# Routing gates of the next expert, split over the first and second layer of a mixture-of-experts kernel

## The chip, the cores and the metric

One core of one Trainium2 chip. The core has a matrix engine (TensorE, with its weight loads shown apart as PEld), VectorE (DVE), ScalarE (ACT), GpSimd (POOL) and SyncE (SP), which each work through their own queue in order and wait for each other through semaphores. The metric is the device time of one execution in microseconds; the median over the runs is compared.

## The reference

Two blocks follow each other. The first is a gated linear recurrence over 768 steps for 4 x 8 heads of width 48; its result, 3072 tokens of 384 numbers, is the input of the second, a router over 8 experts with one expert for each token:

```
xn = x / (np.linalg.norm(x, axis=-1, keepdims=True) + 1e-06)
logits = xn @ en.T / tau
expert_idx = np.argmax(logits, axis=1)
probs = np.exp(logits - logits.max(-1, keepdims=True))
probs /= probs.sum(-1, keepdims=True) + 1e-09
gate_w = probs[np.arange(N), expert_idx]
for e in range(E):
    mask = expert_idx == e
    h = np.maximum(x[mask] @ w1[e], 0.0)
    out[mask] = gate_w[mask, None] * (h @ w2[e])
```

w1 is 384 x 1024 and w2 is 1024 x 384 for each expert. The gate of a token is the softmax value of its largest logit. Since the largest shifted logit is 0, the gate is 1 over the sum of the exponentials. All is float32.

## The kernel before

The first part (up to some 165 us) runs the recurrence in 24 chunks of 128 tokens, computes each token's unnormalised logits, and writes each token's row (384 numbers, 8 logits, its index) to a table in DRAM that is sorted by expert. The part that matters here is the second: the loop over the 8 experts (`run(i)`, then `run_extra(i)`), each with up to three blocks of 128 rows, and a half block of 64 where an expert has more rows than that.

**Rows and weights.** Ahead of `run(i)`, SP fetches the weights of expert i+2 and the rows of expert i+2 into one of three row buffers (`xg_s`). So the rows that `run(i)` prepares, those of expert i+1, were fetched one expert earlier.

**First layer of experts 1 to 7** (`first_layer_blocks`, L995). Three blocks of rows are multiplied by fifteen products of pre-mixed weights and rows in place of eighteen (a Strassen-like scheme). TensorE runs a product into one of four PSUM banks; VectorE adds the bank to a hidden block (`add`, L1019), or ScalarE copies it (L1025, L1027, L1029, L1044, L1046) and applies the relu (L1022). Several products accumulate on a bank that a copy has read in between. Four times (`between`), TensorE transposes a block of the next expert's rows and ScalarE copies it to `xT` (L842, L846). Meanwhile GpSimd mixes the next expert's first weights (`mix_first_weights`, L965), ten operations of 128 x 512.

**Second layer.** The third block is multiplied plainly (`second_layer`, L904, sixteen instructions) and scaled by its gate on ScalarE (L907). The first two blocks are done together in seven products (`second_layer_pair`, L1065), each eight instructions at L1081, on mixed hidden blocks s1 to s4 (`mix_hidden`, L940) and mixed weights t1 to t4 (`mix_weights`, L929). ScalarE reads the first product out of its bank with the gate as a scale (L1093); the third product accumulates on the same bank, so TensorE waits for that reading. Further outputs are read by ScalarE at L1097, L1099 and L1106 and by VectorE in `gated` (L1088). GpSimd scatters the results to the output (L817).

**Rows of the next first layer** (`mix_first_rows`, L967): thirteen VectorE operations that mix the transposed rows of expert i+1.

**Gates of the next expert** (`gates`, L848, through `prepare_gates`, L881). ScalarE squares each block of rows with a running sum (L855, four times) and takes the root (L856). VectorE takes the largest logit (L858), masks the token index (L862, L863), forms the row to scatter to (L864), shifts the logits (L868), adds 1e-6 to the root and inverts it (L869, L870), and multiplies (L871). ScalarE takes Exp (L872). VectorE sums, adds 1e-9 and inverts (L873 to L875). The root and Exp each need a load of ScalarE's function table (L856 and L872, ACT_TABLE_LOAD). The whole is issued behind the last relu of the first layer and the last transposed copy; where it then comes on each engine is left to the scheduler of the language.

**The order of the work.** The program is given to a scheduler that places the instructions of each engine by priority and readiness. Where an order matters, the kernel writes it out: `turn_of(calls)` makes what follows issue behind the calls, `by_dve` chains a call on VectorE to the one before, and `pe_turn` does so on TensorE. ScalarE has no such chain. What the scheduler made of it, on ScalarE in `run(i)` for experts 1 to 6: copies and relus with the four transposed copies between, c21's relu behind the fourth of them, c22's relu, four squares, table load, root, L907, table load, Exp, L1093, L1097, L1099, L1106. On VectorE: the adds, s3, the five operations on the logits, s1, s2, s4, the thirteen row mixes, L869, L870, L871, the sum and what follows it, with `gated` and the next expert's weight mixes t1 to t4 between.

Expert 0 takes another path (its first 256 rows are done early, and a single block is left), and expert 7 prepares no gates.

Of the kernel before, what the change touches and what calls it, by code (L numbers as in the profile page):

```python
# [22 lines left out]
def bc(ap, shape, axis):  # L23
    return ap.unsqueeze(axis).to_broadcast(shape)
# [3 lines left out]
def kernel(  # L28
# [12 lines left out]
    nc = tc.nc  # L41
    B, H, S, D = q.shape
# [115 lines left out]
    def slots(i):  # L158
        return [(t, P) for t in range(blocks_run(i))] + [(blocks_run(i), HALF)]
# [625 lines left out]
    with ExitStack() as c3:  # L785
# [51 lines left out]
        def turn(xg, xT, n, by=None):  # L837
# [7 lines left out]
            pe[:] = [done]  # L845
            return by(xT, px[:, :, 0:n])  # L846

        def gates(xg, gate, col, n, has=None):  # L848

            shp = [P, n, E]  # L850
            l = xg[:, :, LG : LG + E]
            sq = yp.tile([P, NC + 1, 1], FP32, name="gsq")[:, 0:n]
            for t in range(n):
                x2 = yp.tile([P, DM], FP32, name="gx2", bufs=1)
                nc.scalar.activation(x2, xg[:, t, 0:DM], AF.Square, accum_out=sq[:, t])  # L855
            nc.scalar.activation(sq, sq, AF.Sqrt)  # L856
            top = yp.tile([P, NC + 1], FP32, name="gtop")[:, 0:n]
            nc.vector.tensor_reduce(top.unsqueeze(2), l, axis=AX.X, op=ALU.max)  # L858
            none = yp.tile([P, NC + 1, 1], FP32, name="none")[:, 0:n]
            token = xg[:, :, TK : TK + 1]  # L860
            if has is not None:
                nc.vector.tensor_tensor(token, token, has.unsqueeze(2), ALU.mult)  # L862
            nc.vector.tensor_scalar(none, token, 1.0, float(FAR), ALU.is_lt, ALU.mult)  # L863
            nc.vector.scalar_tensor_tensor(  # L864
                out=col.unsqueeze(2), in0=token, scalar=-1.0, in1=none, op0=ALU.add, op1=ALU.add
            )
            sh = yp.tile([P, NC + 1, E], FP32, name="gsh")[:, 0:n]
            nc.vector.tensor_tensor(sh, l, bc(top, shp, 2), ALU.subtract)  # L868
            nc.vector.tensor_scalar(sq, sq, 1e-6, None, ALU.add)  # L869
            nc.vector.reciprocal(sq, sq)  # L870
            nc.vector.tensor_tensor(sh, sh, sq.to_broadcast(shp), ALU.mult)  # L871
            nc.scalar.activation(sh, sh, AF.Exp)  # L872
            nc.vector.tensor_reduce(gate.unsqueeze(2), sh, axis=AX.X, op=ALU.add)  # L873
            nc.vector.tensor_scalar(gate, gate, 1e-9, None, ALU.add)
            return nc.vector.reciprocal(gate, gate)  # L875

        def prepare(i, t, by=None):
            _, n = slots(i)[t]
            return turn(xg_s[i % NXG][:, t], xT_s[i % 2][:, :, t * P : t * P + n], n, by)

        def prepare_gates(i):  # L881
            n = len(slots(i))
# [31 lines left out]

        dve = []

        def by_dve(call, *args):
            with turn_of(dve):
                dve[:] = [call(*args)]  # L919
            return dve[0]  # L920

        def pe_turn():
            return turn_of(pe)
# [13 lines left out]

            return [hT[:, j * FT // 2 : (j + 1) * FT // 2, t * P : (t + 1) * P] for j in range(2)]

        def mix_hidden(hT):  # L940

            (a11, a12), (a21, a22) = (hidden(hT, t) for t in range(2))
            s1, s2, s3, s4 = (hT_m[:, k] for k in range(4))
            for to, x, y, op in (
                (s3, a11, a21, ALU.subtract), (s1, a21, a22, ALU.add),
                (s2, s1, a11, ALU.subtract), (s4, a12, s2, ALU.subtract),
            ):
                by_dve(nc.vector.tensor_tensor, to, x, y, op)

        def halves_w1(w1_t):  # L950

# [40 lines left out]
            v.tensor_tensor(x14, one(b3, 0), x7, ALU.subtract)  # L992
            v.tensor_tensor(x15, one(b1, 1), x6, ALU.add)

        def first_layer_blocks(w1_t, hT, between):  # L995
# [12 lines left out]
            A, B, C, D = (grid(j) for j in (2, 1, 3, 0))  # L1008

            def product(to, left, right, start, stop):  # L1010
                with pe_turn():
                    for f in range(n):
                        pe[:] = [nc.tensor.matmul(  # L1013
                            to[:, f], lhsT=left[:, f * P : (f + 1) * P], rhs=right,
                            start=start and f == 0, stop=stop, skip_group_check=True,
                        )]

            def add(c, p):
                by_dve(nc.vector.tensor_tensor, c, p, c, ALU.add)  # L1019

            def relu(c, p):
                return nc.scalar.activation(c, p, AF.Relu)  # L1022

            product(A, a22, x1, True, False)
            nc.scalar.copy(c21, A)  # L1025
            product(B, g2, y1, True, False)
            nc.scalar.copy(c12, B)  # L1027
# [36 lines left out]

        def second_layer_pair(w2_t, hT, gate, col):  # L1065
# [24 lines left out]
                )  # L1090

            product(a, a11, b11, True, False)
            nc.scalar.mul(u[:, 0], a, g0)  # L1093
# [3 lines left out]
            nc.scalar.mul(u[:, 1], a, g0)  # L1097
            product(d, s1, t1, True, False)
            nc.scalar.mul(u[:, 2], d, g1)  # L1099
# [6 lines left out]
            done_pair[:] = pe[0], nc.scalar.mul(y1[:, 0:m], a, g1)  # L1106
            done_pair.append(scatter(y1, col[:, 1:2]))

        def half_block(w1_t, w2_t, xT, gate, col):
# [31 lines left out]
        def run(i):  # L1141
# [7 lines left out]
            dve[:] = [] if pair else ready  # L1149
            if pair:  # L1150
                mix_weights(w2_t)
                left = list(range(len(nxt)))
                rest = []

                def between():
                    if left:
                        rest[:] = [prepare(i + 1, left.pop(0), nc.scalar.copy)]

                done = first_layer_blocks(w1_t, hT, between)
                if nxt:  # L1160
                    turned = rest[0]
                mix_hidden(hT)
            else:
                for f in range(FT):
                    done = first_layer(w1_t, hT, xT[:, :, 0:n], f, n)
                    if f % 2 == 1 and f // 2 < len(nxt):
                        turned = prepare(i + 1, f // 2)
            if nxt:
                if pair:
                    mix_first_weights(i + 1, nc.gpsimd.tensor_tensor)  # L1170
                with turn_of(dve):
                    mix_first_rows(i + 1)
            if nxt:
                with tc.issue_after(done.ins), tc.issue_after(turned.ins):
                    prepare_gates(i + 1)
            else:

                with turn_of(done_pair):
                    drained.append(nc.gpsimd.drain())
            gate, col = gt_s[i % NG], sx_s[i % NG]  # L1180
            for t in range(2 if pair else 0, blocks_run(i)):
                sent = second_layer(
                    w2_t, hT[:, :, t * P : (t + 1) * P], gate[:, t : t + 1], col[:, t : t + 1],
                    nc.scalar.mul if pair else nc.vector.tensor_scalar_mul,
                )
            if not pair:

# [114 lines left out]
```

## Time and profile before

| | |
|---|---|
| median of 14 runs | 443.21 us (441.22 to 444.58) |
| the profiled execution | 443.46 us |
| its span on the core | 441.6 us |
| granted TensorE clock, mean | 0.979 |
| TensorE matmul busy | 409.6 us, 93% |
| VectorE busy | 285.1 us, 65% |
| ScalarE busy | 196.6 us, 45% |
| GpSimd busy | 222.0 us, 50% |
| expert loop | from about 165 us on |

All times are microseconds from the start of the span unless marked ns. A line of a group reads: line, engine, operation, output and inputs with shapes, how often, then busy time and mean ns of one, then the idle time of that engine just ahead and what ended it. A line of the timeline reads: start, duration, engine, line, operation, and in brackets the idle time ahead and its releaser. The granted clock is the share of full speed that the throttle left TensorE.

### The profile page before, as it was taken

To read this page: it belongs to the slowest core of one execution; us is meant where nothing else is said; L and a number is where in the kernel's file an instruction comes from. 1 tells how busy PE (TensorE), PEld (TensorE's weight loads), DVE (VectorE), ACT (ScalarE), POOL (GpSimd) and SP (SyncE) were. 2 spreads that over 40 slices of the span, in tenths; PEclk is the share of its full clock that TensorE was granted. 3 is DMA by queue.
4 is the path that set the end of the run, shared out by engine and by line. 5 is a ranking of instruction groups with operands and counts; after the bars stand their busy time and mean duration, and the time that the engine had idled before them with its cause. 6 is when DMAs were issued, how large, how long until landed. Compare 5 with 4: busy or idle time off the path is not lost. (4 is left out here: it accounts for less than half of the span.)

```text
span 441.6 us, 11748 instructions
## 1 busy us (share of the span) xinstructions
PE 409.6 (93%) x4570; PEld 363.2 (82%) x4570; DVE 285.1 (65%) x634; ACT 196.6 (45%) x433; POOL 222.0 (50%) x287
## 2 busy tenths in 40 slices
PE   7999999999999999999789889989979997998995
PEld 6798898889889776798689689789959987987984
DVE  7898687797897158636634944951683396397440
ACT  4455454545455344536314614712551471562331
POOL 7546767676655468139216615702831580681101
PEclk9999999999999999999989989989999998999999
DMA  9999999999989326873028009106401900100101
GB/s 140 152 166 150 191 190 189 193 173 205 213 251 387 121 86 185 316 252 124 15 94 296 17 17 340 41 0 242 143 18 50 331 2 16 39 1 16 38 15 40
DMA packets 119375, 60.22 MB, mean 136 GB/s; under 512 B 102287, under 2 KB 113816, under 8 KB 119312
## 3 DMA queue, kind: packets, MB, share of 16 engines
q1 hardware_dynamic: 115208, 49.14, 47.1%
q0 software_dynamic: 3728, 10.16, 6.5%
q8 instruction: 43, 0.70, 0.7%
q14 instruction: 20, 0.16, 0.1%
q10 hardware_dynamic: 376, 0.05, 0.1%
HBM read 49.69 MB, written 11.45 MB: 138 GB/s over the span
## 5 line engine op out<-in xcount | busy, mean ns | idle before, releaser
L817 POOL DMA_INDIRECT out_dram<-y,sx x25 | 26.0, 1040 | 127.2 <-DVE y L1088 64.9
L919 DVE TENSOR_TENSOR hT<-pq,hT 128x512 f32<-128x512 f32 x63 | 43.5, 692 | 52.8 <-PE pq L1013 51.0
L1013 PE MATMUL pq<-xT_m,w_m 128*128 128x128 f32 x560 | 67.8, 277 | 0.0
L1013 PEld LDWEIGHTS pq<-xT_m,w_m 128*128 128x128 f32 x560 | 65.3, 193 | 0.3 <-issue 0.3
L1081 PE MATMUL pq<-w_m,hT_m 128*128 128x192 f32 x168 | 35.8, 381 | 16.5 <-ACT u L1093 16.5
L1081 PEld LDWEIGHTS pq<-w_m,hT_m 128*128 128x128 f32 x168 | 33.9, 227 | 18.3 <-ACT u L1093 18.3
L507 POOL TENSOR_TENSOR qs<-qc,a 128x512 f32<-128x512 f32 x24 | 30.7, 1278 | 35.8 <-DVE a L503 24.2
L904 PE MATMUL pyo<-w,hT 128*128 128x384 f32 x128 | 42.6, 486 | 0.0
L965 POOL TENSOR_TENSOR w_m<-w_m,w 128x512 f32<-128x512 f32 x30 | 41.6, 1393 | 1.4
L1013 PE MATMUL pq<-xT_m,w 128*128 128x128 f32 x280 | 39.3, 281 | 2.4 <-PEq L1199 1.9
L1022 ACT ACTIVATE hT<-hT 128x512 f32<-128x512 f32 x35 | 22.1, 631 | 42.9 <-DVE hT L919 42.5
L1013 PEld LDWEIGHTS pq<-xT_m,w 128*128 128x128 f32 x280 | 35.7, 196 | 3.9 <-issue 3.6
L904 PEld LDWEIGHTS pyo<-w,hT 128*128 128x128 f32 x128 | 23.7, 190 | 14.8
L479 DVE TENSOR_TENSOR_SCAN r<-pa,inr 128x511 f32<-128x511 f32 x24 | 29.2, 1215 | 6.0 <-PE pa L194 5.1
L503 DVE TENSOR_TENSOR_SCAN a<-pa,ini 128x512 f32<-128x512 f32 x24 | 29.4, 1223 | 1.1
L313 POOL DMA_INDIRECT xs<-x,dest x24 | 24.3, 1013 | 8.2 <-issue 4.2
L191 PE MATMUL pyx<-sm,vt 128*64 128x128 f32 x384 | 26.5, 279 | 0.5 <-issue 0.5
L191 PE MATMUL sc<-qs,kr 64*64 64x128 f32 x768 | 26.5, 275 | 0.0
L919 DVE TENSOR_TENSOR w_m<-w 128x768 f32<-128x768 f32 x14 | 13.3, 952 | 20.2 <-PE pq L1081 20.2
L965 POOL TENSOR_TENSOR w_m<-w 128x512 f32<-128x512 f32 x12 | 15.3, 1275 | 19.6 <-PE pq L1013 19.6
L191 PEld LDWEIGHTS pyx<-sm,vt 128*64 128x64 f32 x384 | 20.6, 136 | 5.5 <-issue 5.5
L191 PEld LDWEIGHTS sc<-qs,kr 64*64 64x64 f32 x768 | 20.7, 132 | 4.0 <-issue 3.0
(215 smaller groups left out, 872.1 us busy)
## 6 DMA issues: line engine op xcount, KB each, us to landing
w<-in_moe_w_dram SPq DMA_DIRECT2D x16, 1536.0 KB
kt<-in_k_dram SPq DMA_DIRECT2D x24, 192.0 KB
qt<-in_q_dram SPq DMA_DIRECT2D x24, 192.0 KB
vt<-in_v_dram SPq DMA_DIRECT2D x24, 192.0 KB
xg<-xs SPq DMA_DIRECT2D x22, 196.5 KB
at<-in_alpha_dram SPq DMA_DIRECT2D x24, 168.0 KB
xg<-xs SPq DMA_DIRECT2D x8, 98.2 KB
at<-in_alpha_dram SPq DMA_DIRECT2D x24, 22.5 KB
```

Source lines behind the costliest of these rows:

```text
L191: last["pe"] = nc.tensor.matmul(*args, **kwargs)
L313: ins = nc.gpsimd.indirect_dma_start(out=xs, out_offset=bass.IndirectOffsetOnAxis(ap=rows, axis=0), in_=x, in_offset=None, bounds_check=E ...
L479: nc.vector.tensor_tensor_scan(r[:, L - 2 :: -1], pa[:, L - 1 : 0 : -1], inr[:, L - 2 :: -1], 1.0, ALU.mult, ALU.add,)
L503: d["a_scan"] = by_dve = nc.vector.tensor_tensor_scan(a, pa, ini, 0.0, ALU.mult, ALU.add)
L507: by_pool = nc.gpsimd.tensor_tensor(qs.rearrange("p n t -> p (n t)"), d["qc"], a, ALU.mult)
L817: ins = nc.gpsimd.indirect_dma_start(out=out, out_offset=bass.IndirectOffsetOnAxis(ap=col, axis=0), in_=y, in_offset=None, bounds_check=N - 1,
L904: pe[:] = [nc.tensor.matmul(py, lhsT=hT[:, f], rhs=w2_t[:, f], start=(f == 0), stop=(f == FT - 1),)]
L919: dve[:] = [call(*args)]
L965: by(to, x, y, op)
L1013: pe[:] = [nc.tensor.matmul(to[:, f], lhsT=left[:, f * P : (f + 1) * P], rhs=right, start=start and f == 0, stop=stop, skip_group_check=Tr ...
L1022: return nc.scalar.activation(c, p, AF.Relu)
L1081: pe[:] = [nc.tensor.matmul(to, lhsT=left[:, f], rhs=right[:, f], start=start and f == 0, stop=stop and f == n - 1, skip_group_check=True,)]
```

## The change

`gates` is taken apart into four functions, and in experts 1 to 6 they are called at four places:

- `gates_logits`: the five operations on the logits (largest, mask, index, shift). They are issued on VectorE ahead of the first layer's adds, behind the weight mixes t1 to t4.
- `gates_square`: one squared block. The four are issued on ScalarE within the first layer: behind the first transposed copy, behind c12's relu, and two behind the third transposed copy.
- `gates_norm`: root, addition, inverse, product, Exp. It is issued in `mix_hidden` between s1 and s2; on ScalarE that is behind c22's relu and ahead of L907.
- `gates_end`: sum, addition, inverse. It is issued behind s4 and ahead of the row mixes.

A chain `by_act` writes out ScalarE's order in `run(i)` for experts 1 to 7: the copies, relus, transposed copies, squares, root, Exp and the outputs of the second layer issue as the program lists them. With it the fourth transposed copy comes behind c21's relu. Expert 0 and the early rows keep the old sequence, through a `gates` that calls the four in turn.

```diff
+        def gates_logits(xg, col, n, has=None, by=freely):
...
+            by(v.tensor_reduce, top.unsqueeze(2), l, axis=AX.X, op=ALU.max)
...
+                by(v.tensor_tensor, token, token, has.unsqueeze(2), ALU.mult)
+            by(v.tensor_scalar, none, token, 1.0, float(FAR), ALU.is_lt, ALU.mult)
...
+            by(v.tensor_tensor, sh, l, bc(top, shp, 2), ALU.subtract)
+            return sh, yp.tile([P, NC + 1, 1], FP32, name="gsq")[:, 0:n]
+
+        def gates_square(xg, known, t, by=freely):
+            x2 = yp.tile([P, DM], FP32, name="gx2", bufs=1)
+            by(nc.scalar.activation, x2, xg[:, t, 0:DM], AF.Square, accum_out=known[1][:, t])
+
+        def gates_norm(known, n, by=freely, by_act=freely):
+            sh, sq = known
+            shp = [P, n, E]
+            by_act(nc.scalar.activation, sq, sq, AF.Sqrt)
+            by(nc.vector.tensor_scalar, sq, sq, 1e-6, None, ALU.add)
+            by(nc.vector.reciprocal, sq, sq)
+            by(nc.vector.tensor_tensor, sh, sh, sq.to_broadcast(shp), ALU.mult)
+            by_act(nc.scalar.activation, sh, sh, AF.Exp)
+
+        def gates_end(gate, known, n, by=freely):
+            sh, _ = known
+            by(nc.vector.tensor_reduce, gate.unsqueeze(2), sh, axis=AX.X, op=ALU.add)
+            by(nc.vector.tensor_scalar, gate, gate, 1e-9, None, ALU.add)
+            return by(nc.vector.reciprocal, gate, gate)
...
+        def by_act(call, *args, **kwargs):
+            with turn_of(act):
+                act[:] = [call(*args, **kwargs)]
+            return act[0]
...
-        def mix_hidden(hT):
+        def mix_hidden(hT, between):
...
+            by_dve(v.tensor_tensor, s3, a11, a21, ALU.subtract)
+            by_dve(v.tensor_tensor, s1, a21, a22, ALU.add)
+            between()
+            by_dve(v.tensor_tensor, s2, s1, a11, ALU.subtract)
+            by_dve(v.tensor_tensor, s4, a12, s2, ALU.subtract)
...
             product(D, a13, x11, True, True)
-            nc.scalar.copy(c11, D)
+            by_act(nc.scalar.copy, c11, D)
             between()
+            squares()
             product(A, f2, y2, False, False)
...
             relu(c12, c12)
+            squares()
             product(B, q7, x7, False, False)
-            nc.scalar.copy(c13, B)
+            by_act(nc.scalar.copy, c13, B)
             product(C, q10, x10, True, False)
-            nc.scalar.copy(c23, C)
+            by_act(nc.scalar.copy, c23, C)
             between()
+            squares()
+            squares()
...
             product(a, a11, b11, True, False)
-            nc.scalar.mul(u[:, 0], a, g0)
+            by_act(nc.scalar.mul, u[:, 0], a, g0)
...
                 mix_weights(w2_t)
...
+                if nxt:
+                    known = begin_gates(i + 1, by_dve)
...
+                def norm():
+                    if nxt:
+                        gates_norm(known, len(nxt), by_dve, by_act)
+
+                first_layer_blocks(w1_t, hT, between, squares)
+                mix_hidden(hT, norm)
                 if nxt:
-                    turned = rest[0]
-                mix_hidden(hT)
+                    gates_end(gt_s[(i + 1) % NG][:, 0 : len(nxt)], known, len(nxt), by_dve)
...
-            if nxt:
+            if nxt and not pair:
                 with tc.issue_after(done.ins), tc.issue_after(turned.ins):
                     prepare_gates(i + 1)
```

More of the change, by code (lines that the diff above doesn't have):

```diff
@@ L846, in turn, with freely @@
             return by(xT, px[:, :, 0:n])
+        def freely(call, *args, **kwargs):
+            return call(*args, **kwargs)
         def gates(xg, gate, col, n, has=None):
+            known = gates_logits(xg, col, n, has)
+            for t in range(n):
+                gates_square(xg, known, t)
+            gates_norm(known, n)
+            return gates_end(gate, known, n)
+        def gates_logits(xg, col, n, has=None, by=freely):
+            v = nc.vector
             shp = [P, n, E]
             l = xg[:, :, LG : LG + E]
[L852 to L856, printed above, removed]
             top = yp.tile([P, NC + 1], FP32, name="gtop")[:, 0:n]
-            nc.vector.tensor_reduce(top.unsqueeze(2), l, axis=AX.X, op=ALU.max)
+            by(v.tensor_reduce, top.unsqueeze(2), l, axis=AX.X, op=ALU.max)
             none = yp.tile([P, NC + 1, 1], FP32, name="none")[:, 0:n]
@@ L861, in gates @@
             if has is not None:
[L862 to L865, printed above, removed]
+                by(v.tensor_tensor, token, token, has.unsqueeze(2), ALU.mult)
+            by(v.tensor_scalar, none, token, 1.0, float(FAR), ALU.is_lt, ALU.mult)
+            by(
+                v.scalar_tensor_tensor,
+                out=col.unsqueeze(2), in0=token, scalar=-1.0, in1=none, op0=ALU.add, op1=ALU.add,
             )
             sh = yp.tile([P, NC + 1, E], FP32, name="gsh")[:, 0:n]
[L868 to L875, printed above, removed]
+            by(v.tensor_tensor, sh, l, bc(top, shp, 2), ALU.subtract)
[16 more added lines that the diff above has]
+            return by(nc.vector.reciprocal, gate, gate)
         def prepare(i, t, by=None):
@@ L879, in prepare, with begin_gates @@
             return turn(xg_s[i % NXG][:, t], xT_s[i % 2][:, :, t * P : t * P + n], n, by)
+        def begin_gates(i, by):
+            n = len(slots(i))
+            return gates_logits(
+                xg_s[i % NXG][:, 0:n], sx_s[i % NG][:, 0:n], n, used[:, i, 0:n], by
+            )
         def prepare_gates(i):
@@ L915, with by_dve @@
         dve = []
-        def by_dve(call, *args):
+        act = []
+        def by_dve(call, *args, **kwargs):
             with turn_of(dve):
-                dve[:] = [call(*args)]
+                dve[:] = [call(*args, **kwargs)]
             return dve[0]
+        def by_act(call, *args, **kwargs):
+            with turn_of(act):
+                act[:] = [call(*args, **kwargs)]
+            return act[0]
         def pe_turn():
@@ L938, in hidden @@
             return [hT[:, j * FT // 2 : (j + 1) * FT // 2, t * P : (t + 1) * P] for j in range(2)]
-        def mix_hidden(hT):
+        def mix_hidden(hT, between):
             (a11, a12), (a21, a22) = (hidden(hT, t) for t in range(2))
             s1, s2, s3, s4 = (hT_m[:, k] for k in range(4))
[L944 to L948, printed above, removed]
+            v = nc.vector
+            by_dve(v.tensor_tensor, s3, a11, a21, ALU.subtract)
[3 more added lines that the diff above has]
+            by_dve(v.tensor_tensor, s4, a12, s2, ALU.subtract)
         def halves_w1(w1_t):
@@ L993, in mix_first_rows, with first_layer_blocks @@
             v.tensor_tensor(x15, one(b1, 1), x6, ALU.add)
-        def first_layer_blocks(w1_t, hT, between):
+        def first_layer_blocks(w1_t, hT, between, squares):
             (a11, a12, a13), (a21, a22, a23) = halves_w1(w1_t)
@@ L1021, in relu @@
             def relu(c, p):
-                return nc.scalar.activation(c, p, AF.Relu)
+                return by_act(nc.scalar.activation, c, p, AF.Relu)
             product(A, a22, x1, True, False)
-            nc.scalar.copy(c21, A)
+            by_act(nc.scalar.copy, c21, A)
             product(B, g2, y1, True, False)
-            nc.scalar.copy(c12, B)
+            by_act(nc.scalar.copy, c12, B)
             product(D, a13, x11, True, True)
-            nc.scalar.copy(c11, D)
+            by_act(nc.scalar.copy, c11, D)
             between()
+            squares()
             product(A, f2, y2, False, False)
@@ L1096, in second_layer_pair @@
             product(a, s2, t2, False, False)
-            nc.scalar.mul(u[:, 1], a, g0)
+            by_act(nc.scalar.mul, u[:, 1], a, g0)
             product(d, s1, t1, True, False)
-            nc.scalar.mul(u[:, 2], d, g1)
+            by_act(nc.scalar.mul, u[:, 2], d, g1)
             product(a, s3, t3, False, False)
@@ L1105, in second_layer_pair @@
             product(a, a22, t4, False, True)
-            done_pair[:] = pe[0], nc.scalar.mul(y1[:, 0:m], a, g1)
+            done_pair[:] = pe[0], by_act(nc.scalar.mul, y1[:, 0:m], a, g1)
             done_pair.append(scatter(y1, col[:, 1:2]))
@@ L1151, in run, with squares @@
                 mix_weights(w2_t)
-                left = list(range(len(nxt)))
-                rest = []
+                left, late = list(range(len(nxt))), list(range(len(nxt)))
+                if nxt:
+                    known = begin_gates(i + 1, by_dve)
                 def between():
                     if left:
-                        rest[:] = [prepare(i + 1, left.pop(0), nc.scalar.copy)]
-                done = first_layer_blocks(w1_t, hT, between)
+                        prepare(i + 1, left.pop(0), lambda *args: by_act(nc.scalar.copy, *args))
+                def squares():
+                    if late:
+                        gates_square(xg_s[(i + 1) % NXG], known, late.pop(0), by_act)
+                def norm():
[3 more added lines that the diff above has]
+                mix_hidden(hT, norm)
                 if nxt:
-                    turned = rest[0]
-                mix_hidden(hT)
+                    gates_end(gt_s[(i + 1) % NG][:, 0 : len(nxt)], known, len(nxt), by_dve)
             else:
@@ L1172, in run @@
                     mix_first_rows(i + 1)
-            if nxt:
+            if nxt and not pair:
                 with tc.issue_after(done.ins), tc.issue_after(turned.ins):
                     prepare_gates(i + 1)
-            else:
+            if not nxt:
                 with turn_of(done_pair):
@@ L1183, in run @@
                     w2_t, hT[:, :, t * P : (t + 1) * P], gate[:, t : t + 1], col[:, t : t + 1],
-                    nc.scalar.mul if pair else nc.vector.tensor_scalar_mul,
+                    (lambda *args: by_act(nc.scalar.mul, *args)) if pair
+                    else nc.vector.tensor_scalar_mul,
                 )
```

## The prediction

> **What bounds the kernel now.** I read the page first. TensorE is busy for 409.6 of 441.6 us (93%), so what can be won is its idle time and its slow time. Next came the list of who waited for whom on TensorE, longest first:
>
> ```profile
> PE pq L1081 <- ACT u L1093: 16.5, 6, 2.9
> PE pq L1013 <- PEq L1199: 1.9, 1, 1.9
> ```
>
> One wait holds 16.5 us: six times, 2.9 us at most, at the second layer's products (L1081), until ScalarE has read the first product out of its bank (L1093). Third, the groups by shape on ScalarE tell why ScalarE is late there:
>
> ```profile
> L872 ACT ACTIVATE gsh<-gsh 128x32 f32<-128x32 f32 x7 | 1.6, 229 | 19.4 <-DVE gsh L871 19.4
> ```
>
> ScalarE sat idle for 19.4 us ahead of the gates' Exp, for VectorE's multiplication L871. Fourth, the timeline of one expert (its second-layer pair starts at 323.50 us) shows the chain; columns are start, duration, engine, line:
>
> ```profile
> 323.50 2.76 PE L1081 MATMUL pq<-w,hT 128*128 128x192 f32 x16
> 324.30 1.28 ACT L872 ACT_TABLE_LOAD   x1
> 324.88 0.42 DVE L979 TENSOR_TENSOR xT_m<-xT 128x256 f32<-128x256 f32 x1
> ...
> 327.71 0.28 DVE L993 TENSOR_TENSOR xT_m<-xT,xT_m 128x128 f32<-128x128 f32 x1
> ...
> 328.32 0.19 DVE L871 TENSOR_TENSOR gsh<-gsh,gsq 128x32 f32<-128x32 f32 x1
> 328.55 0.23 ACT L872 ACTIVATE gsh<-gsh 128x32 f32<-128x32 f32 x1 [2.96 <-DVE gsh L871]
> 328.68 0.40 ACT L1093 ACTIVATE u<-pq,gt 128x192 f32<-128x192 f32 x1
> 329.14 4.17 PE L1081 MATMUL pq<-w_m,hT_m 128*128 128x192 f32 x24 [2.87 <-ACT u L1093]
> ```
>
> ScalarE issues in order: Exp stands ahead of L1093 and waits for three small VectorE operations that stand behind thirteen row mixes (L979 to L993). Last, the windows of this stage, from the first product of the pair (L1081) to the start of the next first layer, for experts 1 to 7; columns are length, busy time and count of PE, PEld, DVE, ACT, POOL, granted clock, DMA:
>
> ```profile
> 211.71:225.63 13.92, 11.04 (x57) 10.75 (x56) 9.12 (x28) 3.25 (x6) 1.54 (x2) 0.88 0.03 12
> 249.28:263.19 13.91, 11.04 (x57) 10.75 (x56) 9.08 (x28) 3.25 (x6) 1.51 (x2) 0.88 0.04 15
> 283.45:297.37 13.92, 11.04 (x57) 10.75 (x56) 9.10 (x28) 3.25 (x6) 1.49 (x2) 0.88 0.04 15
> 323.50:335.78 12.28, 9.41 (x57) 9.04 (x56) 9.09 (x28) 3.25 (x6) 1.29 (x1) 1.00 0.04 16
> 362.07:375.98 13.91, 11.04 (x57) 10.75 (x56) 9.09 (x28) 3.25 (x6) 1.37 (x2) 0.88 0.03 13
> 396.24:407.80 11.56, 9.41 (x58) 9.05 (x56) 8.46 (x26) 3.25 (x6) 1.29 (x2) 1.00 0.04 14
> 426.90:436.00 9.10, 9.10 (x57) 8.96 (x55) 1.25 (x3) 1.85 (x4) 1.39 (x2) 1.00 0.06 21
> ```
>
> The last line is expert 7, which prepares no gates: seven products back to back, 1.30 us apart, 9.10 us. (Its end is the last product's start, 434.70, plus 1.30.) It is the yardstick. The other six run 4.82, 4.81, 4.82, 3.18, 4.81 and 2.46 us longer, 24.90 us together. So the wait costs more than 16.5: in four of six the granted clock is 0.88, and the 24 matmul instructions behind the wait take 5.85 us where the other two show 4.17.
>
> **The price of a stall.** 24.90 = 16.5 of wait, plus 4 x 1.63 = 6.5 of slow clock (PE busy 11.04 against 9.41), plus 6 x 0.31 = 1.9 of refilling. Windows of 0.4 us show when the clock changes (columns: length, PE busy and count, clock, DMA); those in between stand at 0.50:
>
> ```profile
> 218.40:218.80 0.40, 0.40 (x4) 0.85 0.00 0
> ...
> 222.00:222.40 0.40, 0.40 (x4) 0.89 0.00 0
> ...
> 228.80:229.20 0.40, 0.40 (x5) 0.65 0.15 41
> ...
> 232.00:232.40 0.40, 0.40 (x4) 0.59 1.07 440
> ```
>
> [...]
>
> [...]
>
> **What the change does.** TensorE, GpSimd and SP issue the same instructions in the same order in both builds, so no DMA and no scatter moves; nothing is added or removed on ScalarE or VectorE either, only moved. The times below are in the frame of the expert shown.
>
> (a) *Exp and L1093.* The row mixes now stand behind the gates. After the last relu (c22) ScalarE loads a table (1.28), does Sqrt (0.20), loads again (1.28) and does Exp. The fourth transposed copy (0.21 from start to start) moves from before c21's relu to before c22's, so that relu ends at 319.37 instead of 319.16; Sqrt is done at about 320.9, the second load at about 322.2. VectorE goes s3, s1, then the three norm operations. s1 needs c22, starts at 319.4 and takes 1.64 beside GpSimd's weight mixes (what each mix took at 393.67 and 395.34; 0.69 in expert 7, where GpSimd stands), so 321.05. The three norm operations take 0.64 at their own rate. Held behind GpSimd, as L862 and L863 were (1.13 and 1.23 instead of 0.16 and 0.17), each could cost 1.07 more. I take one held, the scalar addition, which is nearest to L863; the broadcast product is nearest to L868, which took 0.18 there. So Exp goes at about 322.8, at worst at 324.2. L907's copy of the third block's result waits for TensorE until 323.70 anyway, and L1093 follows at 325.06, 0.26 behind its product. TensorE wants that bank again at 326.10, L1093 ends at 325.46: 0.6 us spare. The wait falls away in all six experts: -24.90.
>
> (b) *The squares.* Four per expert, 0.65 us apart (319.06, 319.69, 320.34, 320.99). The first goes into 1.88 us in which ScalarE waited ahead of c11's relu; three and four end at about 315.4, before c13's relu at 316.25. The second stands ahead of the copy of c13, which moves from 312.00 to 312.65 and ends at 313.24; TensorE accumulates onto that bank at 313.54 (its product before starts at 312.65, 0.89 apart). 0.3 us spare, so nothing; with that cover gone at most 6 x 0.35 = 2.1 us.
>
> (c) *The logits' five operations* go to VectorE's queue behind the last weight mix of the expert before. VectorE stands 3.09 us there ahead of the first add, 3.39 us where the half block is skipped; the five take 0.65 alone (182.48 to 183.13) and 2.69 beside GpSimd. Nothing. Their rows are on chip: the transposes read them at 306.31 without a wait.
>
> (d) *VectorE behind the gates.* This is what is late next. s2 and s4, three operations for the rows' sums (0.6), the row mixes (3.03) and the first gated output (0.42) must be through when the first weight mix is released, at 328.96 (0.26 behind the fourth product). From there VectorE is tight: mix 0.96, mix 0.96, gated 0.41, done at 331.24, and the seventh product wants that bank at 331.30. With GpSimd done at 323 or so I get 322.8 + 1.0 + 0.7 + 0.6 + 3.03 + 0.42 = 328.55: 0.4 us spare. If s2 is held until GpSimd is through, at 323.7 (its three mixes took 5.08 at 391.36, 4.34 elsewhere), the sum is 323.7 + 0.69 + 0.69 + 0.6 + 3.03 + 0.42 = 329.1, 0.15 late; if those mixes are stretched by another half, 0.7 late. So 0 to 0.7 per expert; a gain is excluded, since the yardstick has no wait. I take 0.05, near the low end, as the rows give 0.4 spare: +0.3.
>
> Sum: -24.9 + 0.3 = -24.6. The profiled execution took 443.46 us (span 441.6), 0.25 above the median of 443.21, so I take off nothing for that: 418.9. The slow clock behind the branch at 228 us, 1.6 us (5.83 from 228.37 to 234.20 against 4.23 from 304.19 to 308.42), depends on where the grid lies when the gap of 1.9 us comes, about even odds, and the gap comes 4.8 us earlier; a quarter of it off gives 418.5.
>
> **Rivals.** *Forecast, 0.74*: wait and slow clock both go, 418.5, its own range 416 to 421.
>
> *VectorE is the new wait, 0.15*: step (d) is late by 0.7 to 1.5 us per expert, at the seventh product. For it: VectorE is busy for 9.09 us in the stage of 12.28, and the stage is to take 9.1. Against it: it leaves 0.64 of norm work to the stage before, and L1093 no longer shares the delay. [...]
>
> *It does only half of what it says, 0.06*: Exp is held until the bank is late, a wait of about 1.2 us stays in each expert without slow clock, 6 x 1.5: 427.5. Against it the 0.6 us spare with Exp already at its worst.
>
> *Slower, 0.03*: VectorE now reads the next expert's rows at the head of its queue before the first layer's adds, and ScalarE before its relus. Should those rows land late, adds, banks and TensorE wait. It decides from 24.6 / 6 = 4.1 us of delay behind the covers; 6 us would give 443.5 + 6 x (6 - 4.1) = 455. For it: once, at 187.27, this reduction waited 2.80 us for its rows. Against it: the others were fetched an expert (34 us or more) earlier. The remaining 0.02 is no change at all, should a stall of like size form elsewhere.
>
> **Range and chances.** From 415.5 (no slow clock behind the branch, no lateness) to 424.5, which takes in most of the second case. A difference under 0.2% (0.9 us) can't be told from no change. Faster 0.95, same 0.02, slower 0.03.
>
> **What would show it.** Right: L1081's wait for L1093 gone; the stage windows near 9.1 to 9.2 us at clock 1.00 in all experts; Exp ahead of L907's copy; no new wait at L1013. Wrong: TensorE waiting for VectorE's gated output at the seventh product (d), for the copy of c13 (b), or a granted clock under 1.00 in these windows without a gap.

## The result, and the profile after

The kernel after the change took 418.1 us (median of 13 runs, 417.57 to 420.37), the kernel before it 442.55 (62 runs): a ratio of 0.9458, 95% interval 0.944 to 0.9476, or 24.45 us less. The forecast was 418.5. Here and below, ratios and intervals leave out executions that the record marks as slow: none of these, two of the ten of e8, and one of 2278.5 us of the kernel before in the second group.

The profiled execution of the kernel after is a short one: 416.29 us, below all 13 timed runs, with a span of 414.3. First, from its page, the span, the busy time of each engine and the granted clock over 40 slices:

```profile
span 414.3 us, 11758 instructions
PE 400.2 (97%) x4570; PEld 355.3 (86%) x4570; DVE 283.0 (68%) x634; ACT 195.7 (47%) x433; POOL 222.4 (54%) x287
PEclk9999999999999999999999999999999999999999
```

TensorE's busy time fell from 409.6 to 400.2 with the same products in it. 8.1 us of that lie in the six stages below (62.98 before, 54.84 after): 6.5 of slow clock and 1.6 of refilling behind the waits; the slow clock behind the branch (1.6) is the rest, to 0.3. The clock now stands at 9 (0.9 or more) in every slice. TensorE's share rose to 97%, since the idle time fell too. The list of who waited for whom on TensorE, longest first (total, times, longest):

```profile
PE pw L191 <- POOL ident masks.py:199: 1.6, 1, 1.6
PE pyo L1157 <- DVE y L933: 1.4, 1, 1.4
```

The 16.5 us at the pair's products (L1081 before, L1119 now) are gone. So is, in this execution, the gap of 1.9 us at the branch. In second place stands a wait that was 0.40 us before: expert 0's half block (L1157) waits for VectorE to take y out of its bank (L933). We come back to both.

The timeline of expert 4, the expert the prediction worked in. Its pair starts at 306.55; add 16.95 for the prediction's frame. The ordering helpers now give most of these instructions their own lines, L947 on VectorE and L952 on ScalarE, so they are told apart by their tiles.

```profile
301.66 4.75 POOL L999 TENSOR_TENSOR w_m<-w_m,w 128x512 f32<-128x512 f32 x3
302.44 1.28 ACT L952 ACT_TABLE_LOAD   x1
302.46 1.49 DVE L947 TENSOR_TENSOR hT_m<-hT 128x512 f32<-128x512 f32 x1 [0.19 <-ACT hT L952]
303.98 1.12 DVE L947 TENSOR_SCALAR gsq<-gsq 128x4 f32<-128x4 f32 x1
305.13 0.18 DVE L947 RECIPROCAL gsq<-gsq 128x4 f32<-128x4 f32 x1
305.34 1.12 DVE L947 TENSOR_TENSOR gsh<-gsh,gsq 128x32 f32<-128x32 f32 x1
306.49 0.23 ACT L952 ACTIVATE gsh<-gsh 128x32 f32<-128x32 f32 x1 [1.24 <-DVE gsh L947]
306.55 2.76 PE L1119 MATMUL pq<-w,hT 128*128 128x192 f32 x16
306.75 0.58 ACT L952 ACTIVATE y<-pyo,gt 128x384 f32<-128x384 f32 x1
308.05 0.42 ACT L952 ACTIVATE u<-pq,gt 128x192 f32<-128x192 f32 x1 [0.72 <-PE pq L1119]
309.15 4.06 PE L1119 MATMUL pq<-w_m,hT_m 128*128 128x192 f32 x24
311.22 0.41 DVE L1126 SCALAR_TENSOR_TENSOR y<-pq,gt,u 128x192 f32<-128x192 f32 x1
311.95 0.96 DVE L947 TENSOR_TENSOR w_m<-w 128x768 f32<-128x768 f32 x1 [0.32 <-PE pq L1119]
```

The first line is GpSimd's last three weight mixes, which end at 306.41. Exp (306.49) starts before the pair does. The reading of the first product (308.05) waited for its own product and for nothing else, and the third product follows the second at 309.15 with no bracket: no wait. The last line is where VectorE is tight: it stood for 0.32 us until its weight mix was released, so it was that much early.

The windows of this stage for experts 1 to 7, from the pair's first product to the next first layer; columns are those of the prediction (length, busy time and count of PE, PEld, DVE, ACT, POOL, granted clock, DMA):

```profile
212.27:221.41 9.14, 9.14 (x58) 9.07 (x57) 8.42 (x24) 2.02 (x5) 1.06 (x1) 1.00 0.06 20
241.66:250.80 9.14, 9.14 (x57) 9.07 (x56) 8.41 (x24) 2.01 (x5) 1.05 (x1) 1.00 0.06 21
271.06:280.20 9.14, 9.14 (x58) 9.07 (x57) 8.41 (x24) 2.02 (x5) 1.05 (x1) 1.00 0.07 23
306.55:315.69 9.14, 9.14 (x58) 9.07 (x57) 8.41 (x24) 2.01 (x5) 1.05 (x1) 1.00 0.06 22
342.02:351.16 9.14, 9.14 (x57) 9.07 (x56) 8.43 (x24) 2.03 (x5) 1.06 (x1) 1.00 0.05 19
371.42:380.56 9.14, 9.14 (x57) 9.07 (x56) 8.42 (x24) 2.02 (x5) 1.05 (x1) 1.00 0.05 18
399.66:408.76 9.10, 9.10 (x57) 8.96 (x55) 1.25 (x3) 1.84 (x4) 1.39 (x2) 1.00 0.06 21
```

Six stages of 9.14 us, PE busy for all of each, stand against the 9.10 of expert 7. Before they took 13.92, 13.91, 13.92, 12.28, 13.91 and 11.56. The span's 27.3 us divide so:

| part of the span | change, us |
|---|---|
| up to expert 1's stage (start 211.71 before, 212.27 after) | +0.56 |
| the six stages | -24.66 |
| from expert 1's stage to expert 2's (23.65 before, 20.25 after) | -3.40 |
| the other stretches between stages, and the tail | +0.20 |

The 3.40 us are, to 0.1, the gap at the branch (1.9) and the slow clock behind it (1.6), which this execution happened not to have. So it is the -24.66 of the stages that is set beside the 24.45 of the medians; how often the executions without a profile have the gap or the slow clock is not on record.

### The profile page after: what moved, and what is told of

Its sections match the earlier page's. It is cut to its first block, busy times and chain, and to the rows that moved or that the text cites. A ratio compares the mean times of both kernels' runs of the same rounds, so it can differ in the third digit from the quotient of the medians.

```text
span 414.3 us, 11758 instructions
## 1 busy us (share of the span) xinstructions
PE 400.2 (97%) x4570; PEld 355.3 (86%) x4570; DVE 283.0 (68%) x634; ACT 195.7 (47%) x433; POOL 222.4 (54%) x287
## 5 line engine op out<-in xcount | busy, mean ns | idle before, releaser
L817 POOL DMA_INDIRECT out_dram<-y,sx x25 | 24.8, 991 | 103.7 <-DVE y L1126 42.2
L947 DVE TENSOR_TENSOR hT<-pq,hT 128x512 f32<-128x512 f32 x63 | 43.4, 692 | 46.4 <-PE pq L1047 44.7
L999 POOL TENSOR_TENSOR w_m<-w_m,w 128x512 f32<-128x512 f32 x30 | 43.2, 1448 | 1.4
L1047 PE MATMUL pq<-xT_m,w 128*128 128x128 f32 x280 | 38.4, 277 | 0.6
L952 ACT ACTIVATE hT<-hT 128x512 f32<-128x512 f32 x35 | 22.1, 631 | 31.2 <-DVE hT L947 31.1
L1119 PE MATMUL pq<-w_m,hT_m 128*128 128x192 f32 x168 | 28.4, 326 | 0.0
L1119 PEld LDWEIGHTS pq<-w_m,hT_m 128*128 128x128 f32 x168 | 27.5, 190 | 0.0
L489 ACT COPY qc<-pq 128x512 f32<-128x512 f32 x24 | 14.0, 584 | 21.4 <-PE pq L194 19.0
```

Source lines behind the costliest of these rows:

```text
L817: ins = nc.gpsimd.indirect_dma_start(out=out, out_offset=bass.IndirectOffsetOnAxis(ap=col, axis=0), in_=y, in_offset=None, bounds_check=N - 1,
L947: dve[:] = [call(*args, **kwargs)]
L952: act[:] = [call(*args, **kwargs)]
L999: by(to, x, y, op)
L1047: pe[:] = [nc.tensor.matmul(to[:, f], lhsT=left[:, f * P : (f + 1) * P], rhs=right, start=start and f == 0, stop=stop, skip_group_check=Tr ...
L1119: pe[:] = [nc.tensor.matmul(to, lhsT=left[:, f], rhs=right[:, f], start=start and f == 0, stop=stop and f == n - 1, skip_group_check=True,)]
```

## The experiments

The kernels ran in three groups (e1 to e4, e5 to e8, e9 and e10), each on one chip beside the kernel before, whose median there was 442.69, 435.55 and 436.78 us. Since the chips differ by 1.6%, only ratios are compared across groups. The expectations are told on the scale of a kernel before of 442.55 us; "scaled" is a ratio times that.

**e1: the row mixes again ahead of the norm.** Everything else of the change stays: the split, the squares inside the first layer, ScalarE's written order.

```diff
...
-                mix_hidden(hT, norm)
+                mix_hidden(hT, lambda: None)
+                if nxt:
+                    with turn_of(dve):
+                        dve[:] = [mix_first_rows(i + 1)]
+                norm()
...
-                with turn_of(dve):
-                    mix_first_rows(i + 1)
+                if not pair:
+                    with turn_of(dve):
+                        mix_first_rows(i + 1)
```

> The changed kernel with one thing undone: on VectorE the thirteen row mixes come ahead of the norm operations again; squares and logits stay early and ScalarE's order stays written out. Theory (ScalarE's in-order queue holds the first product's reading behind Exp, and Exp behind the row mixes): the wait of TensorE at the second layer's pair comes back in six experts, about 2.8 us each, since Exp now also stands ahead of the third block's output; with the slow clock behind it 440 to 445 us. Rival (the early squares and the written ScalarE order are what helped): 418 to 425 us.

Measured: 440.65 us, ratio 0.9958 (0.9932 to 0.9983), scaled 440.7, within the expected 440 to 445. The longest wait of TensorE in its profile, and Exp and the reading in expert 4 (the pair starts at 318.47):

```profile
PE pq L1119 <- ACT u L952: 15.7, 6, 2.6
```

```profile
322.15 0.15 DVE L947 TENSOR_SCALAR gsq<-gsq 128x4 f32<-128x4 f32 x1
322.77 0.23 ACT L952 ACTIVATE gsh<-gsh 128x32 f32<-128x32 f32 x1 [5.62 <-DVE gsh L947]
323.37 0.41 ACT L952 ACTIVATE u<-pq,gt 128x192 f32<-128x192 f32 x1
```

The wait is back in all six experts. The stages took 12.04, 12.03, 13.72, 12.01, 13.67 and 13.67 us; in three of the six the 24 instructions behind the wait took 5.85 us instead of 4.17. So splitting the gates and moving squares and logits is worth 2 us of 24 while the row mixes stand between the root and Exp.

**e2: the kernel before with one order written out.** Nothing is split; only the row mixes are issued behind the whole of the gates.

```diff
-                with turn_of(dve):
-                    mix_first_rows(i + 1)
+                if not pair:
+                    with turn_of(dve):
+                        mix_first_rows(i + 1)
...
-                    prepare_gates(i + 1)
+                    got = prepare_gates(i + 1)
+                if pair:
+                    with turn_of(dve), turn_of([got]):
+                        mix_first_rows(i + 1)
```

> The kernel before with one order changed: the row mixes issue behind the gates; squares, logits and the rest stay where they were, nothing is split. Theory: most of the gain is here. Exp at about 325.6 in the frame of the expert that starts its pair at 323.50, the reading of the first product ends at 326.6 (0.6 us late), and VectorE releases the bank of the seventh product about 1.1 us late: 1.0 to 1.4 us per expert, no slow clock, 424 to 427 us. Rival (the split is needed, half of it brings nothing): above 435 us.

Measured: 421.11 us, ratio 0.9511 (0.9459 to 0.9564), scaled 420.9, below the expected 424 to 427. Its wait at the pair, and its timeline around Exp (the pair starts at 309.86):

```profile
PE pq L1081 <- ACT u L1093: 1.6, 5, 0.3
```

```profile
311.25 0.16 DVE L869 TENSOR_SCALAR gsq<-gsq 128x4 f32<-128x4 f32 x1
311.66 0.19 DVE L871 TENSOR_TENSOR gsh<-gsh,gsq 128x32 f32<-128x32 f32 x1
311.89 0.23 ACT L872 ACTIVATE gsh<-gsh 128x32 f32<-128x32 f32 x1 [1.10 <-DVE gsh L871]
312.49 0.41 ACT L1093 ACTIVATE u<-pq,gt 128x192 f32<-128x192 f32 x1
```

In the prediction's frame Exp came at 325.53 and L1093 was through at 326.54, and TensorE waited 0.31 to 0.34 us for the bank. Five stages took 9.85 to 9.87 us, 0.72 above those of the change; the sixth took 9.15. In the sixth no logits stand between s3 and s1: as in the kernel before, the scheduler placed the logits one expert early, and their last reduction comes at 341.65, ahead of the fifth pair (346.02). (The sixth wait of the kernel before, without them too, was 2.15 us and not 2.87.) The expected loss was too large at its second place: the third product starts 3.09 behind the pair's start (2.60 after the change), but the seventh only 5.38 behind the third (5.20). The mechanism is as expected, its size smaller. One order written out brings most of the gain (21.6 us by the medians). By its stages the split brings 3.6 us more; the two ratios alone don't tell them apart.

**e3: the four squares behind the last relu; e4: the five logits operations between s3 and s1.** Each takes one cover away that the prediction named.

```diff
-                first_layer_blocks(w1_t, hT, between, squares)
+                first_layer_blocks(w1_t, hT, between, lambda: None)
+                for _ in nxt:
+                    squares()
```

> The changed kernel with the four squares back behind the last relu, nothing else undone. Theory: the root comes 2.6 us later, Exp at about 324.8 in that frame, which the reading of the first product still bears; VectorE's row mixes come about 1.0 us later than in the changed kernel, 0.6 to 0.7 us past their spare time, paid at the seventh product: 6 x 0.65, 421 to 423.5 us, no slow clock. Rival (moving the squares into the first layer is worth nothing): 417.5 to 419.5 us; rival (it is what matters): above 430 us.

Measured: 419.59 us, ratio 0.9464 (0.9392 to 0.9535), scaled 418.8: by its time it lies where the rival "worth nothing" put it. The stages, of 9.30 to 9.32, lie 0.17 above those of the change instead of 0.65, 1.0 us in all. Exp came where it was expected (310.66, in the prediction's frame 324.66). The first weight mix started 0.19 late and the seventh product 0.11.

```diff
...
-                    known = begin_gates(i + 1, by_dve)
+                    sq = yp.tile([P, NC + 1, 1], FP32, name="gsq")[:, 0 : len(nxt)]
+                    known = [None, sq]
...
             by_dve(v.tensor_tensor, s3, a11, a21, ALU.subtract)
+            logits()
             by_dve(v.tensor_tensor, s1, a21, a22, ALU.add)
```

> The changed kernel with the five logits operations back between s3 and s1 on VectorE, beside GpSimd's mixes. Theory: they take 2.7 us there, VectorE's row mixes end about 1.1 us later than in the changed kernel, 0.75 us past the release of the first weight mix, paid at the seventh product: 6 x 0.75, 421.5 to 424 us. Rival (VectorE has time enough in this stage): 417.5 to 419.5 us.

Measured: 416.63 us, ratio 0.9438 (0.9358 to 0.9517), scaled 417.7; stages of 9.40 to 9.42, 0.28 above instead of 0.75. The total hides this loss. Like the profile of the change its profile has no gap at the branch, and without logits ahead of it y is taken out in time: the wait for y is gone, and expert 1's stage starts at 210.77, 1.50 us earlier than after the change. The timeline of its VectorE says why the loss is small:

```profile
301.54 1.13 DVE L947 TENSOR_TENSOR xg<-xg,used 128x4 f32<-128x4 f32 x1
302.70 1.19 DVE L947 TENSOR_SCALAR none<-xg 128x4 f32<-128x4 f32 x1
304.00 1.26 DVE L947 TENSOR_TENSOR gsh<-xg,gtop 128x32 f32<-128x32 f32 x1
305.19 0.68 DVE L947 TENSOR_TENSOR hT_m<-hT 128x512 f32<-128x512 f32 x1
305.80 0.16 DVE L947 TENSOR_SCALAR gsq<-gsq 128x4 f32<-128x4 f32 x1
306.20 0.19 DVE L947 TENSOR_TENSOR gsh<-gsh,gsq 128x32 f32<-128x32 f32 x1
```

Three logits operations took 1.13 to 1.26 us beside GpSimd's mixes. But GpSimd's mixes ended at 305.22, and s1 behind them took 0.68 instead of 1.49, the norm operations 0.16 and 0.19 instead of 1.12 each. In the profiles of e4 and of the kernel after, each of these operations that took over 1.1 us began while GpSimd's mixes ran, so what was lost early wasn't lost again later. e3 and e4 show that the rival "VectorE is the new wait" is a real mechanism, with its place at the seventh product (TensorE's weight load waits for VectorE there, 0.24 us in e3 and 0.33 in e4), and that the expectations put its price at more than twice what it is.

**e5: VectorE's old order, but Exp moved behind the pair's last output on ScalarE.** The row mixes again stand ahead of the norm, as in e1. If Exp at the head of ScalarE's queue is what costs, and not the row mixes, the gain must stay.

```diff
...
-            by_act(nc.scalar.activation, sh, sh, AF.Exp)
+            if then is None:
+                by_act(nc.scalar.activation, sh, sh, AF.Exp)
...
-                mix_hidden(hT, norm)
+                mix_hidden(hT, lambda: None)
                 if nxt:
-                    gates_end(gt_s[(i + 1) % NG][:, 0 : len(nxt)], known, len(nxt), by_dve)
+                    with turn_of(dve):
+                        dve[:] = [mix_first_rows(i + 1)]
+                norm()
...
                 second_layer_pair(w2_t, hT, gate, col)
+                if nxt:
+                    by_act(nc.scalar.activation, known[0], known[0], AF.Exp)
+                    gates_end(gt_s[(i + 1) % NG][:, 0 : len(nxt)], known, len(nxt))
```

> VectorE's old order again (row mixes ahead of the norm), but Exp moved behind the pair's last output on ScalarE, the sums behind it; squares and logits early as in the changed kernel. Theory (what cost was Exp standing in ScalarE's queue ahead of the reading, not the row mixes as such): the wait stays away, VectorE ends its row mixes and norm before the first weight mix is released, 417 to 420.5 us, the upper end if the table load delays the first copies of the next first layer. Rival (the row mixes must go behind the gates): 438 to 445 us.

Measured: 412.26 us, ratio 0.9455 (0.9384 to 0.9527), scaled 418.4, within the expected 417 to 420.5. The window of expert 4, and from its timeline L1093's reading and the first VectorE instruction of the norm:

```profile
301.26:310.40 9.14, 9.14 (x58) 9.07 (x57) 7.99 (x23) 1.84 (x4) 1.27 (x2) 1.00 0.06 22
```

```profile
302.76 0.42 ACT L953 ACTIVATE u<-pq,gt 128x192 f32<-128x192 f32 x1 [0.72 <-PE pq L1120]
304.94 0.16 DVE L948 TENSOR_SCALAR gsq<-gsq 128x4 f32<-128x4 f32 x1
```

The norm begins 3.68 us behind the pair's start (301.26), and nobody waits: the reading goes at 302.76, 1.50 behind the start, as after the change. In e1 the norm begins just as late, 3.68 behind the start (322.15 and 318.47), and there TensorE waits 2.6 us in each expert. The two differ in Exp's place on ScalarE, with the sums that follow Exp. This settles the cause: the row mixes cost only because Exp, which waits for what stands behind them, is ahead of the reading in ScalarE's queue.

**e6: the change without ScalarE's written order.**

```diff
-            with turn_of(act):
-                act[:] = [call(*args, **kwargs)]
-            return act[0]
+            return call(*args, **kwargs)
```

> The changed kernel without ScalarE's written order: the scheduler places two squares in the first layer and two behind c22's relu, the rest as before. Theory: the root comes about 1.3 us later, VectorE's spare 0.3 us is used and little more: 418 to 420.5 us. Rival (the written order is a part of the gain): above 423 us.

Measured: 413.51 us, ratio 0.9483 (0.9409 to 0.9557), scaled 419.7, within the expected 418 to 420.5; all six stages 9.14, one new wait of 0.7 us in expert 1's first layer. The written order isn't what brings the gain; whether it is worth the microsecond between the ratios can't be told from these runs.

**e7 and e8: the change, with seven or eleven copies ahead of L1093's reading on ScalarE.** The copies of 128 x 384 are added and used by nobody. They make the same wait from another source, in two sizes: one of about 1.3 us, one of the old size.

```diff
...
             product(a, a11, b11, True, False)
+            if nxt:
+                idle = yp.tile([P, 4, DM], FP32, name="idle", bufs=1)
+                for k in range(7):
+                    by_act(nc.scalar.copy, idle[:, k % 4], blank[:, 0:DM])
             by_act(nc.scalar.mul, u[:, 0], a, g0)
...
```

> The changed kernel with seven copies of 128x384 from a constant into a spare tile on ScalarE, ahead of the reading of the first product, in the six experts: a stall of TensorE made to measure, about 1.3 us each at 0.39 us a copy. They compute nothing. [...] Rival (each stall slows the clock in proportion): 430 us or more.

> The same with eleven copies, a stall of about 2.9 us each, as long as in the kernel before. Theory: 6 x 3.2 of stall and refill, and four or five intervals of slow clock at 1.63 us: 443 to 446 us, the time of the kernel before. [...]

Measured: e7 420.63 us, ratio 0.9642 (0.9571 to 0.9713), scaled 426.7, below the rival's 430 and 1.0 below the 427.7 that the price of a stall gives (418.1 + 6 x (1.3 + 0.3)); e8 440.55 us (439.22 over those that its ratio counts), ratio 1.009 (1.0044 to 1.0137), scaled 446.5, just above the expected 443 to 446. Windows of e7 for experts 1 and 4, then of e8 for the same two, and e8's line of waits:

```profile
207.32:217.99 10.67, 9.40 (x57) 9.04 (x56) 8.41 (x24) 4.78 (x12) 1.04 (x1) 1.00 0.05 17
305.47:316.14 10.67, 9.40 (x58) 9.04 (x56) 8.42 (x24) 4.79 (x12) 1.06 (x1) 1.00 0.05 18
```

```profile
206.86:220.82 13.96, 11.05 (x58) 10.75 (x57) 8.49 (x24) 6.41 (x16) 1.24 (x2) 0.88 0.04 13
314.87:327.19 12.32, 9.41 (x58) 9.04 (x57) 8.51 (x24) 6.43 (x16) 1.05 (x1) 1.00 0.04 16
```

```profile
PE pq L1119 <- ACT u L952: 17.6, 6, 3.0
```

Six waits of 1.26 us cost 1.53 each (10.67 against 9.14), with the clock at 1.00 in the windows; PE busy goes from 9.14 to 9.40, which the prediction calls refilling. Six waits of 2.91 to 3.02 cost 3.2 to 4.9 each. Behind four of them, of 2.91 and 2.92, the 24 instructions take 5.85 us (in expert 1 the clock of the stage is 0.88 and PE busy 11.05 instead of 9.41); behind the other two, of 2.91 and 3.02, they take 4.17, as in e7. These are the stages of the kernel before, made anew without its gates. So the three terms of the 24.9, wait, refilling and slow clock, belong to the wait and not to anything else that was moved. (The profiled execution of e8 is its fastest, 435.43. The others were granted less clock, 0.961 to 0.976 in the mean against 0.979, which fits more stages with slow clock; without profiles of them that isn't shown.)

**e9 and e10: the longer wait for y.** VectorE has, ahead of y, a logits operation of expert 2 that waits for its rows. The kernel before has it too; after the change the rows and y come later and TensorE comes earlier. First the two lines of before, then those of after:

```profile
187.27 0.19 DVE L858 TENSOR_REDUCE gtop<-xg 128x4 f32<-128x32 f32 x1 [2.80 <-DMA xg<-xs]
188.55 1.73 PE L1119 MATMUL pyo<-xT,w 128*64 128x64 f32 x48 [0.40 <-DVE y L907]
```

```profile
187.79 0.19 DVE L947 TENSOR_REDUCE gtop<-xg 128x4 f32<-128x32 f32 x1 [3.76 <-DMA xg<-xs]
188.47 0.61 DVE L933 TENSOR_SCALAR y<-pyo,gt 128x384 f32<-128x384 f32 x1
189.13 1.71 PE L1157 MATMUL pyo<-xT,w 128*64 128x64 f32 x48 [1.44 <-DVE y L933]
```

e9 lets VectorE take y out first; e10 is the kernel after the change, unaltered, on the same chip.

```diff
...
-            by(y, py, gate)
+            last_y[:] = [by(y, py, gate)]
...
-                    known = begin_gates(i + 1, by_dve)
+                    with turn_of(last_y if i == 1 else []):
+                        known = begin_gates(i + 1, by_dve)
```

> The changed kernel with one order added: for expert 1 alone, VectorE takes expert 0's last output out of its bank ahead of expert 2's logits. In the profile of the changed kernel that output waits behind the logits for rows from DRAM, and TensorE for its bank: 1.44 us (0.40 in the kernel before). Theory: that wait goes, 0.4 to 1.4 us less than the changed kernel. Rival (the wait moves to the rows' next reader): no difference.

> The changed kernel once more, for the comparison with the one order added, on the same chip and against the same runs: 418.1 us.

Measured: e9 411.11 us, ratio 0.9423 (0.9383 to 0.9463), scaled 417.0; e10 412.05 us, ratio 0.9444 (0.9403 to 0.9486), scaled 417.9. The wait of L1157 for y was 0.87 us in e10's profile and is not there in e9's, and the transposes, the rows' next reader on TensorE, wait no longer for them than in e10 (0.2 us against 0.4). The medians differ by 0.94 us in the same direction, but the intervals overlap: the trace shows the wait gone, the times don't show a gain. It is a lead, and no version here is shown to beat the kernel after the change.

## Why the prediction was right

The time came from the likeliest case, by its mechanism. Point by point:

- **The wait, the refilling and the slow clock** (24.9 us in six stages): measured 24.66 less. e7 measures the refilling (0.27 per stall against 9.14, where 0.31 against 9.10 had been taken); e8 measures the slow clock (1.64 of PE busy against 1.63, and again in four stalls of six).
- **Exp (a)**: at 323.44 in the prediction's frame, not 322.8. Two of the three norm operations, the scalar addition and the broadcast product, took 1.12 us each beside GpSimd's mixes; one had been taken as held, with L868's 0.18 as the measure for the product (in e4 L868's operation itself took 1.26). What made it harmless is the cover that was named: L907's copy waits for TensorE until 323.70 either way. L1093 went at 325.00; 325.06 had been said.
- **The squares (b)**: nothing, as said; the first layers show no new wait. e3 prices the alternative at 0.17 per stage.
- **The logits (c)**: "their rows are on chip" holds for the later experts and fails once, ahead of expert 1, where the reduction waited 3.76 us for its rows, y stood behind it, and TensorE with it. That is the mechanism of the rival "slower", but it was there before the change as well, with 2.80 and 0.40 us. Of the 1.04 us more at L1157, 0.45 is TensorE reaching the bank earlier (its products start at 186.08, before at 186.53) and the rest y coming later (188.47, before 187.88), mostly with the rows; that the change made the rows late isn't shown. Expert 1's stage starts 0.56 later.
- **VectorE behind the gates (d)**: gated ended at 328.58 in that frame, 328.55 had been said; 0.32 spare before the weight mix against 0.4. The excess of the stages over the yardstick was 6 x 0.04 = 0.24, with 0.3 taken. The agreement is partly luck: the norm was through 0.6 us later than taken (323.41 against 322.8), and s2, s4 and the sums behind it took 1.84 us instead of 2.3, with GpSimd through by then (323.36). e3 and e4 show what it costs when the spare is used up: 0.17 and 0.28 us per stage, where the range's upper end, 424.5, allows 6 x 1.0 on 418.5.
- **The branch**: a quarter of the slow clock (1.6 us) had been taken off, for the place of a grid and "about even odds". That was the author's estimate, and no run shows the term. In the profile of the kernel after neither the gap nor the slow clock appears; in e10, the same kernel, there is a gap of 1.86 and the clock behind it is 1.00. Of the seven profiles with a gap of 1.86 to 2.36 us, only that of the kernel before (1.90) shows slow clock behind it: after two instructions of 0.46 us the next eight take 1.68 us there, and 1.06 in the six others. The term was a guess about a matter that varies from execution to execution, and the 0.4 us lie within the spread.
- **Standing and the clock**: how long TensorE stood doesn't tell by itself what the clock did. Waits of 2.91 us in e8 were followed by 24 instructions in 5.85 us three times and in 4.17 once, and the one of 3.02 by 4.17; a gap of 1.90 was followed by slow clock in the kernel before, and one of 2.36 in e6 was not. What decides it isn't shown. The forecast didn't hang on it, since the waits went away.

What stays open is the gap where expert 1 jumps over its skipped half block. The profiles show TensorE waiting there 1.86 to 2.36 us in the kernel before and in e1, e2, e3, e6, e9 and e10, 0.57 in e5, and not at all in the kernel after, e4, e7 and e8. It probably accounts for the distance of the profiled execution of after (416.29) from its median: timed executions with the same mean clock of 0.998 have spans of 415.9 to 416.3 against its 414.3, and e10, with the gap, lies on its median (412.06 and 412.05). But e4, without the gap, lies near its median too (416.86 and 416.63), so this isn't shown. What makes the gap come or stay away was not tried.

## What to carry to other kernels

In a queue that is worked through in order, as ScalarE's was here (up to 2.6 us of wait per expert in e1, none in e5), every instruction is as urgent as the most urgent one behind it: when the bounding engine waits for a short reading, look at what stands ahead of that reading on its engine and for whom *it* waits, and either feed that one earlier (e2) or put it behind (e5). Price a stall by its stage against a twin without the stall, not by its wait alone: here 1.26 us cost 1.53, and 2.9 us cost 3.2, or 4.8 where the clock fell. When something is moved forward in a queue, check the first iteration by itself: its data may not have come yet.

## What the runs showed of the hardware

Small VectorE operations took different times beside GpSimd's mixes: in the kernel after, the scalar addition of 128 x 4 and the product of 128 x 32 took 1.12 us each (0.16 and 0.19 in e4, when GpSimd was through), while the reciprocal of 128 x 4 between them took 0.18 both times. The two that took 1.12 us each ended within 0.05 us of the end of one of GpSimd's mixes. The logits' shift of 128 x 32 took 0.18 us in the kernel before, where it began at 320.29 and GpSimd's last three mixes ran from 318.63 to 322.97, and 1.26 in e4, where it began at 304.00 and they ran from 300.93 to 305.22. What decides which operation is the long one isn't shown.

A stall of 1.26 us in e7, with the clock at 1.00, still adds 0.26 us of TensorE busy time (9.40 against 9.14). By the profile, which models the ends of matmuls, 0.16 of it lies ahead of the wait: the first two products take 2.76 us, of which the third covers the last 0.16 when it follows at once (2.60). The other 0.10 lies behind it: from the third product to the end of the stage 6.64 instead of 6.54.

Two loads of ScalarE's function table with a root between them follow one another closely in the kernel after: the load at 302.44 takes 1.28 us and the next activation, the root, begins at 303.74, 0.02 us behind its end.
